# Local attention's 1e-9 as a constant row of the value product, and one bank for the last pooled queries' scores

## The chip, the cores and the metric

The kernel runs on one core of a Trainium2 chip. The metric is the device time of one execution in microseconds, taken as the median of several runs of the same program. Five engines work beside each other, each with its own instruction stream in a fixed order: TensorE (PE in the rows; its weight loads are PEld), VectorE (DVE), ScalarE (ACT), GpSimd (POOL) and SyncE (SP), which here issues most of the DMAs. Matmuls write PSUM, which has eight banks of 128 partitions by 512 fp32 columns.

## The reference

Two attentions over the same q, k and v (4 batches, 8 heads, 576 positions, head size 64) are added, and the sum goes through two token-and-channel mixers. The changed part is in the attentions:

```python
def sm_attn(qq, kk, vv):                      # over 144 pooled positions
    s = scale * np.matmul(qq, kk.transpose(0, 1, 3, 2))
    s = s - np.max(s, axis=-1, keepdims=True)
    a = np.exp(s)
    a = a / (np.sum(a, axis=-1, keepdims=True) + 1e-09)
    return np.matmul(a, vv)
...
out_up = np.repeat(out_d, factor, axis=2)     # factor 4
mask = np.abs(pos[:, None] - pos[None, :]) < factor
scores = np.where(mask, scores, -1000000000.0)
scores = scores - np.max(scores, axis=-1, keepdims=True)
attn = np.exp(scores)
attn = attn / (np.sum(attn, axis=-1, keepdims=True) + 1e-09)
out_local = np.matmul(attn, v)
return (out_up + out_local).astype(np.float32)
```

After it come `x + relu(x @ w_ch1) @ w_ch2` style mixers and a product with sines and cosines; the change does not touch them.

## The kernel before

The attention works on pairs of heads and on quads (two pairs, that is four heads). There are 16 pairs (`n`) and 8 quads (`Q`).

`quad_front(Q)` is the pooled attention of a quad. Its first step multiplies 32-query blocks of pooled q with pooled k: for pair `p` and head `j` of the pair, four blocks `c` of 32 queries fill the 128 partitions of the score tile `sd`, bank `j`, columns `p * 144` (L434). 144 pooled queries are four blocks of 32 and 16 more; the last 32 queries of each head are done by a further matmul (L443) into the columns 288 to 431 of bank `j`, on the partitions of block `2 j + p`. Head `j` reads partitions 64 j to 64 j + 63 of q and k, so the two heads use the two halves of TensorE's rows. The second step takes the maxima on VectorE: one reduce for the four main blocks (L452) and two for the last queries, one for each bank, on 64 partitions each (L460). The third takes the exponentials on ScalarE: four main ones (L468) and two on 64 partitions (L473). Then follow transposes on TensorE (L477, L482), copies on ScalarE, the product with the pooled values (L493 to L500) into the tile `od`, the division on VectorE (L504 to L507), a store, and a load that repeats the rows (`xu`).

`pair_local(n)` is the local attention of a pair in blocks of 32 queries by W = 38 keys. The scores (L533) are reduced and shifted on VectorE (L545, L546) into one of two buffers `pbuf`, of which 38 of 64 columns are used; the rest was set to zero at the start (L328). After the exponential (L553) the transposes (L558) bring a whole buffer, keys on partitions, back to PSUM. The product with the values (L568) has 38 rows of keys; a 65th value column of ones gives the sum of the exponentials. VectorE adds 1e-9 to that sum (L577), takes the reciprocal (L578) and multiplies (L582).

`token_mix`, `token_hidden`, `token_out` are the first mixer over positions (tiles `t1`, `t2`), `mix` the one over channels (tiles `c1`, `c2`).

PSUM is shared by two pools. `big` has two tiles of two banks each (`wide(...)`): all score, transpose and local output tiles. `mmp` has four tiles of one bank (tag `mm`): `od`, `t1`, `t2`, `c1` and `c2`. A tile of a pool waits until an earlier tile's last reader has released its bank.

The order of the work is written out by hand in `ORDER` (L33 to L84): each entry runs one step (the code up to the next `yield`) of a generator. `F` is quad_front, `L` pair_local, `T` token_mix, `E` token_hidden, `U` token_out (which copies `t2` out on ScalarE, L653), `C` mix, `H` and `O` its hidden and output steps. Each engine executes its instructions in exactly that order. Line 42 of it begins:

```
P13 T2 P12 L9 L10 C0 A6 F5 X4 C0 U2.0 L10 U2.0 X5 U2.0 C0 X3 F5 X6 F4 F5 C0 A7 F4 ...
```

Here the first `F5` is the first step of quad 5, and the first `F4` is the seventh step of quad 4, the division.

Of the kernel before, what the change touches and what calls it, by code (L numbers as in the profile page):

```python
# [12 lines left out]
F32 = mybir.dt.float32  # L13
# [5 lines left out]
AF = mybir.ActivationFunctionType  # L19
ALU = mybir.AluOpType  # L20
AX = mybir.AxisListType
# [72 lines left out]
B, H, S, D = 4, 8, 576, 64  # L94
DM = H * D
SD = S // 4
DTOK = 256
# [4 lines left out]
W = 38  # L102
# [12 lines left out]
def kernel(  # L115
# [16 lines left out]
    act, dve, pool, pe, sp = nc.scalar, nc.vector, nc.gpsimd, nc.tensor, nc.sync  # L132

    dram = ctx.enter_context(tc.tile_pool(name="dram", bufs=1, space=DRAM))
    od_d = [[dram.tile([32, 4, DTOK], F32, name=f"od_{b}_{h}") for h in range(2)] for b in range(B)]
    ot_d = [[dram.tile([32, DTOK], F32, name=f"ot_{b}_{h}") for h in range(2)] for b in range(B)]
# [148 lines left out]
    mmp = ctx.enter_context(tc.tile_pool(name="mma", bufs=8 - 2 * WIDE, space=PSUM))  # L285
# [7 lines left out]
    def wide(name):  # L293
        return big.tile([128, 2, 512], F32, tag="big", name=name)
# [28 lines left out]
    def constants():  # L323
        sp.dma_start(fixed, consts)
        yield
        pool.memset(zero, 0.0)
        for t in pbuf:
            pool.memset(t, 0.0)  # L328
        yield
        act.copy(id16, idt)  # L330
        yield
# [50 lines left out]
    def load_values(n):  # L382
        b, p4 = divmod(n, 4)
        vw = sb2.tile([128, 18, 65], F32, tag="vw", name=f"vw_{b}_{p4}")
        for rows in (slice(0, 32), slice(32, W)):
            for j in range(2):
                sp.dma_start(vw[64 * j + rows.start : 64 * j + rows.stop], vloc[b, p4, j, rows])
        values[n] = vw
        yield
# [35 lines left out]
    def quad_front(Q):  # L425
        b, hh = divmod(Q, 2)
        at = f"{b}_{hh}"
        qkd = pooled[Q]
        qd, kd = qkd[:, :, 0], qkd[:, :, 1]
        sd = wide(f"sd_{at}")  # L430
        for p in range(2):
            for c in range(4):
                for j in range(2):
                    pe.matmul(  # L434
                        sd[32 * c : 32 * c + 32, j, p * SD : (p + 1) * SD],
                        qd[64 * j : 64 * j + 64, p, 32 * c : 32 * c + 32],
                        kd[64 * j : 64 * j + 64, p, :],
                        start=True,
                        stop=True,
                    )  # L440
            for j in range(2):
                c = 2 * j + p
                pe.matmul(  # L443
                    sd[32 * c : 32 * c + 32, j, 2 * SD : 3 * SD],
                    qd[64 * j : 64 * j + 64, p, SD - 32 : SD],
                    kd[64 * j : 64 * j + 64, p, :],
                    start=True,
                    stop=True,
                )
        yield  # L450
        mx = sb2.tile([128, 5], F32, tag="mxd", name=f"mxd_{at}")
        dve.tensor_reduce(  # L452
            out=mx[:, 0:4].rearrange("p (j a) -> p j a", j=2),
            in_=sd[:, :, 0 : 2 * SD].rearrange("p j (a n) -> p j a n", a=2),
            axis=AX.X,
            op=ALU.max,
        )
        for j in range(2):
            r = slice(64 * j, 64 * j + 64)
            dve.tensor_reduce(out=mx[r, 4:5], in_=sd[r, j, 2 * SD : 3 * SD], axis=AX.X, op=ALU.max)  # L460
        yield
        scale = 1.0 / (16.0 * math.sqrt(D))
        act.activation(mx, mx, AF.Copy, scale=-scale)
        pd = sb1.tile([128, 5, SD], F32, tag="pd", name=f"pd_{at}")
        for j in range(2):
            for p in range(2):
                i = 2 * j + p
                act.activation(  # L468
                    pd[:, i, :], sd[:, j, p * SD : (p + 1) * SD], AF.Exp, scale=scale, bias=mx[:, i : i + 1]
                )  # L470
        for j in range(2):
            r = slice(64 * j, 64 * j + 64)
            act.activation(pd[r, 4, :], sd[r, j, 2 * SD : 3 * SD], AF.Exp, scale=scale, bias=mx[r, 4:5])  # L473
        yield
        pt = wide(f"pdt_{at}")
        for i in range(5):
# [9 lines left out]
        act.copy(pts[:, 4:7].rearrange("p a n -> p (a n)"), pt[:, 1, 0:384])  # L486
        yield
        vs, vl = pooled[Q, "v"]
        od = mmp.tile([128, 512], F32, tag="mm", name=f"od_{at}")

        rows = [slice(32 * c, 32 * c + 32) for c in range(4)]
        for r in rows:
            pe.matmul(od[r, 0:260], pts[:, 5, r], vl.rearrange("p h d -> p (h d)"), start=True, stop=False)  # L493
# [12 lines left out]
        ods = sb1.tile([128, 5, 64], F32, tag="ods", name=f"ods_{at}")  # L506
        dve.tensor_tensor(out=ods, in0=odv[:, :, 0:64], in1=rd.to_broadcast([128, 5, 64]), op=ALU.mult)  # L507
        yield
        base, tail = od_d[b][hh], ot_d[b][hh]
        sp.dma_start(base.rearrange("s k n -> k s n"), ods[:, 0:4, :].rearrange("p c d -> p (c d)"))  # L510
        sp.dma_start(tail.rearrange("s (c d) -> c s d", c=4), ods[:, 4, :])
        yield
        xu = sb1.tile([128, NB, DTOK], F32, tag="xu", name=f"xu_{b}_{hh}")
        xus[Q] = xu
        src = base.rearrange("s k n -> s (k n)").unsqueeze(1).to_broadcast([32, 4, 4 * DTOK])
        sp.dma_start(xu[:, 0:4].rearrange("p k n -> p (k n)"), src)
        src = tail[16:32].unsqueeze(1).to_broadcast([16, 4, DTOK])
        for j in range(2):
            sp.dma_start(xu[64 * j : 64 * j + 64, 4], src)
        yield  # L520
# [1 line left out]
    def pair_local(n):  # L522
# [9 lines left out]
        for i, j, r, g in groups:  # L532
# [15 lines left out]
            in0=sv,  # L548
# [17 lines left out]
        for i, j, r, g in groups:  # L566
            h = 64 * j
            pe.matmul(  # L568
                o[r : r + 32, 5 * j + i // 2],
                pts[h : h + W, i // 2, r : r + 32],  # L570
                vw[h : h + W, g, :],
                start=True,
                stop=True,
            )
        yield
        rl = sb2.tile([128, 2 * NB, 1], F32, tag="rl", name=f"rl_{at}")
        dve.tensor_scalar(out=rl, in0=o[:, :, 64:65], scalar1=1e-9, scalar2=None, op0=ALU.add)  # L577
        dve.reciprocal(out=rl, in_=rl)  # L578
        if p == 0:
            xs_of[n // 2] = sb2.tile([128, 2, NB, 128], F32, tag="x", name=f"x_{at}")  # L580
        x = xs_of[n // 2]
# [797 lines left out]
def _layout(x):  # L1379
# [6 lines left out]
    vpad = np.zeros((B, 4, 2, S + 6, 65), f)  # L1386
    vpad[:, :, :, 3 : 3 + S, 0:64] = v.reshape(B, 4, 2, S, D)
    vpad[..., 64] = 1.0
    vloc = vpad[:, :, :, np.arange(W)[:, None] + 32 * np.arange(18), :]

    vg = np.ones((B, 2, 2, 2, SD, 4, 65), f)
    vg[..., 0:64] = v.reshape(B, 2, 2, 2, SD, 4, D).transpose(0, 1, 3, 2, 4, 5, 6)
# [42 lines left out]
```

## Time and profile before

| what | value |
| --- | --- |
| time, median of 3 runs | 685.61 us (683.41 to 687.0) |
| profiled execution | 681.57 us, of which the span of its instructions 679.8 us |
| PE (matmul) busy | 655.9 us, 96% of the span, 7320 instructions |
| PEld busy | 626.7 us, 92% |
| DVE busy | 521.0 us, 77%, 952 instructions |
| ACT busy | 321.2 us, 47%, 632 instructions |
| POOL busy | 98.5 us, 14%, 92 instructions |
| chain that ended last | PE 84%, DVE 8%, DMA 3%, ACT 3% |

The attention runs in the first 190 us or so; the channel mixers and the last stage follow. Matmuls are pipelined, so a busy PE is not PE at its peak. A row's idle time in brackets is that of the engine just before the first of its instructions, with what ended it; "issue" means that the engine waited for nothing that the profile shows.

### The profile page before, as it was taken

Reading aid. Unit: us, or ns where it says so; the run is one execution under the profiler, and the core shown is the slowest. Engines: PE = TensorE matmul, PEld = TensorE weight load, DVE = VectorE, ACT = ScalarE, POOL = GpSimd, SP = SyncE. Lnnn points to the kernel's source line nnn. Section 1 sums busy time; section 2 is a strip of 40 time slices with the busy share of each in tenths; the row PEclk is TensorE's granted clock in tenths of the full one; section 3 lists DMA queues with packets and bytes.
Section 4 is the critical chain, followed back from the end, with each engine's and each line's share of the span. In section 5 each row is a group of like instructions: output and inputs, shape, how many; then the busy total and the mean of one; then the engine's idle time right before and its main releaser. Section 6 shows DMA issues by size and latency. Waiting matters only on the chain.

```text
span 679.8 us, 17390 instructions
## 1 busy us (share of the span) xinstructions
PE 655.9 (96%) x7320; PEld 626.7 (92%) x7320; DVE 521.0 (77%) x952; ACT 321.2 (47%) x632; POOL 98.5 (14%) x92
## 2 busy tenths in 40 slices
PE   6769899999999999999999999999999999999997
PEld 4558789889999999999999999999999998998997
DVE  5889998697542888998988867677898748857837
ACT  4566667455341674535434523154647326527311
POOL 3223322305000333300101200012000000000000
PEclk9889999999999999999999999999999999999999
DMA  8787788757343785527263762699410330140202
GB/s 282 239 277 229 250 274 260 252 179 238 110 157 104 242 293 186 202 62 207 66 194 127 209 142 85 238 324 279 130 63 0 112 114 1 62 141 1 71 1 69
DMA packets 93022, 109.93 MB, mean 162 GB/s; under 512 B 46881, under 2 KB 69537, under 8 KB 92945
## 3 DMA queue, kind: packets, MB, share of 16 engines
q1 hardware_dynamic: 92080, 106.08, 49.6%
q0 software_dynamic: 864, 2.75, 1.0%
q8 instruction: 57, 0.93, 0.6%
q14 instruction: 21, 0.16, 0.1%
HBM read 79.13 MB, written 29.69 MB: 160 GB/s over the span
## 4 chain that ended last, share of the span: by engine, by line
PE 84%; DVE 8%; DMA 3%; ACT 3%; SPq 1%; issue 1%; DVEq 0%; ACTq 0%
PE y L157 6%; PE y L158 6%; PE y L159 6%; PE c L157 4%; PE c L158 4%; PE c L159 4%; PE c L699 4%; PE c L702 4%; PE c L700 4%; PE c_p L905 3%; PE c_p L902 3%; PE c_p L903 3%; PE t L157 2%; PE t L159 2%; PE t L158 2%; DMA qk<-qkT 2%
## 5 line engine op out<-in xcount | busy, mean ns | idle before, releaser
L157 PE MATMUL y<-wrh,zh 128*128 128x288 f32 x256 | 75.0, 296 | 0.8 <-ACT zh L151 0.8
L158 PE MATMUL y<-wrl,zh 128*128 128x288 f32 x256 | 74.9, 296 | 0.0
L159 PE MATMUL y<-wrh,zl 128*128 128x288 f32 x256 | 72.9, 295 | 0.0
L219 POOL TENSOR_TENSOR ww<-ww,raw 128x512 int32<-128x512 int32 (+2 forms) x30 | 41.1, 1373 | 159.2 <-DMA raw<-w_ch 52.5
L157 PEld LDWEIGHTS y<-wrh,zh 128*128 128x128 f32 x256 | 48.0, 188 | 1.1 <-ACT zh L151 1.1
L158 PEld LDWEIGHTS y<-wrl,zh 128*128 128x128 f32 x256 | 48.0, 188 | 0.0
L159 PEld LDWEIGHTS y<-wrh,zl 128*128 128x128 f32 x256 | 47.3, 188 | 0.0
L219 POOL TENSOR_TENSOR raw<-raw 128x512 int32<-128x512 int32 (+2 forms) x16 | 20.0, 1249 | 136.7 <-DVE raw L215 74.1
L1212 DVE TENSOR_TENSOR cx<-y,cx 128x288 f32<-128x288 f32 x32 | 14.4, 455 | 30.3 <-PE y L159 29.9
L151 ACT CAST cuh<-cx 128x288 fp32r<-128x288 f32 (+1 forms) x16 | 8.8, 553 | 57.5 <-DVE cx L1212 57.4
L157 PE MATMUL th<-thh,cxh 128*128 128x512 f32 (+1 forms) x92 | 31.6, 343 | 0.0
L158 PE MATMUL th<-thl,cxh 128*128 128x512 f32 (+1 forms) x92 | 31.6, 343 | 0.0
L159 PE MATMUL th<-thh,cxl 128*128 128x512 f32 (+1 forms) x92 | 31.6, 343 | 0.0
L199 ACT ACTIVATE ww<-raw 128x512 f32<-128x512 f32 (+2 forms) x30 | 19.5, 649 | 25.3 <-DVE c1l L223 9.4
L921 DVE SCALAR_TENSOR_TENSOR g<-c,g 128x384 fp32r<-128x384 f32 x40 | 21.1, 550 | 12.9 <-ACT g L918 12.9
L918 ACT ACTIVATE g<-c 128x384 fp32r<-128x384 f32 x40 | 19.1, 490 | 24.4 <-PE c L159 24.3
L201 ACT ACTIVATE raw<-raw 128x512 int32<-128x512 uint32 (+3 forms) x46 | 29.5, 640 | 0.0
L568 PE MATMUL o<-vw,plt 38*32 38x65 f32 x1280 | 18.0, 236 | 6.9 <-issue 3.6
L929 DVE TENSOR_TENSOR ut<-c,ut 128x384 f32<-128x384 f32 x32 | 17.1, 551 | 9.8 <-PE c L702 9.8
L568 PEld LDWEIGHTS o<-vw,plt 38*32 38x32 f32 x1280 | 15.4, 110 | 9.6 <-issue 4.8
L157 PE MATMUL t<-w2h,h 128*128 128x256 f32 (+1 forms) x64 | 21.6, 337 | 0.0
L157 PE MATMUL c<-uh,c1h 128*128 128x384 f32 x64 | 21.4, 334 | 0.0
(390 smaller groups left out, 2266.6 us busy)
## 6 DMA issues: line engine op xcount, KB each, us to landing
raw<-w_ch SPq DMA_DIRECT2D x27, 512.0 KB
qk<-qkT SPq DMA_DIRECT2D x16, 582.0 KB
xT<-ut SPq DMA_DIRECT2D x12, 768.0 KB
vd<-vtok SPq DMA_DIRECT2D x8, 650.0 KB
vw<-vloc SPq DMA_DIRECT2D x32, 146.2 KB
uT<-us SPq DMA_DIRECT2D x16, 288.0 KB
ut<-uT SPq DMA_DIRECT2D x6, 768.0 KB
ut<-xT SPq DMA_DIRECT2D x6, 768.0 KB
```

The lines of the kernel that those rows point to most:

```text
L157: pe.matmul(out, lh, rh, start=start, stop=False, skip_group_check=again)
L158: pe.matmul(out, lh, rl, start=False, stop=False, skip_group_check=again)
L159: pe.matmul(out, ll, rh, start=False, stop=stop, skip_group_check=again)
L201: act.activation(f, words[:, :, 0], AF.Copy, scale=2.0**-29)
L219: pool.tensor_tensor(out=w.bitcast(I32), in0=w.bitcast(I32), in1=f, op=ALU.add)
L568: pe.matmul(o[r : r + 32, 5 * j + i // 2], pts[h : h + W, i // 2, r : r + 32], vw[h : h + W, g, :], start=True, stop=True,)
L699: pe.matmul(ps[:, 0:MIX], h[:, cb % 2, d], h1, start=cb == cbs[0], stop=False)
L700: pe.matmul(ps[:, 0:MIX], l[:, cb % 2, d], h1, start=False, stop=False)
L702: pe.matmul(ps[:, 0:MIX], weight[cb // 2][2][:, cb % 2, d], h2, start=False, stop=cb == cbs[-1])
L902: pe.matmul(ps[:, 0:MIX], h[:, cb % 2, d], h1, start=cb == cbs[0], stop=False)
L903: pe.matmul(ps[:, 0:MIX], l[:, cb % 2, d], h1, start=False, stop=False)
L921: dve.scalar_tensor_tensor(out=h2, in0=ps, scalar=0.0, in1=h1.bitcast(F32), op0=ALU.max, op1=ALU.subtract)
```

## The change

The local attention's buffers `pbuf` get a 39th column of ones, set once at the start; the transposes make it a 39th row, and the values on the host get a 39th row of keys that is zero but for 1e-9 in the column of ones. The product over 39 rows so gives the sum plus 1e-9, and L577 goes. The value loads take one more row in their second part.

In quad_front the last 32 queries' scores of all four heads go into the columns 368 to 511 of the bank of `od`, which is taken at the first step for that; their maxima are one reduce over 128 partitions, their exponentials one instruction. The product with the pooled values later uses the columns 0 to 324 of the same bank.

```diff
@@ constants
         for t in pbuf:
             pool.memset(t, 0.0)
+            pool.memset(t[:, :, W : W + 1], 1.0)
@@ load_values
-        for rows in (slice(0, 32), slice(32, W)):
+        for rows in (slice(0, 32), slice(32, W + 1)):
@@ quad_front
         sd = wide(f"sd_{at}")
+        od = mmp.tile([128, 512], F32, tag="mm", name=f"od_{at}")
+        tail = od[:, 512 - SD : 512]
...
                 pe.matmul(
-                    sd[32 * c : 32 * c + 32, j, 2 * SD : 3 * SD],
+                    tail[32 * c : 32 * c + 32],
                     qd[64 * j : 64 * j + 64, p, SD - 32 : SD],
...
-        for j in range(2):
-            r = slice(64 * j, 64 * j + 64)
-            dve.tensor_reduce(out=mx[r, 4:5], in_=sd[r, j, 2 * SD : 3 * SD], axis=AX.X, op=ALU.max)
+        dve.tensor_reduce(out=mx[:, 4:5], in_=tail, axis=AX.X, op=ALU.max)
...
-        for j in range(2):
-            r = slice(64 * j, 64 * j + 64)
-            act.activation(pd[r, 4, :], sd[r, j, 2 * SD : 3 * SD], AF.Exp, scale=scale, bias=mx[r, 4:5])
+        act.activation(pd[:, 4, :], tail, AF.Exp, scale=scale, bias=mx[:, 4:5])
...
-        od = mmp.tile([128, 512], F32, tag="mm", name=f"od_{at}")
@@ pair_local
-                pts[h : h + W, i // 2, r : r + 32],
-                vw[h : h + W, g, :],
+                pts[h : h + W + 1, i // 2, r : r + 32],
+                vw[h : h + W + 1, g, :],
...
-        dve.tensor_scalar(out=rl, in0=o[:, :, 64:65], scalar1=1e-9, scalar2=None, op0=ALU.add)
-        dve.reciprocal(out=rl, in_=rl)
+        dve.reciprocal(out=rl, in_=o[:, :, 64:65])
@@ the values' layout on the host
-    vloc = vpad[:, :, :, np.arange(W)[:, None] + 32 * np.arange(18), :]
+    vloc = np.zeros((B, 4, 2, W + 1, 18, 65), f)
+    vloc[:, :, :, 0:W] = vpad[:, :, :, np.arange(W)[:, None] + 32 * np.arange(18), :]
+    vloc[:, :, :, W, :, 64] = 1e-9
```

## Rows read from the trace of the kernel before

**Rows 1.** Busy time by stretches: stretch, length, each engine, granted clock, DMA share, GB/s.

```profile
58.00:79.00 21.00, 18.64 (x531) 16.40 (x532) 20.16 (x40) 16.01 (x40) 9.25 (x8) 1.00 0.77 256
79.00:102.00 23.00, 22.10 (x701) 19.46 (x699) 21.84 (x38) 15.17 (x31) 6.43 (x6) 1.00 0.85 270
102.00:190.00 88.00, 87.61 (x1809) 81.18 (x1795) 65.59 (x124) 47.35 (x109) 22.38 (x26) 1.00 0.64 211
190.00:460.00 270.00, 270.00 (x1584) 269.49 (x1583) 206.72 (x367) 117.87 (x214) 40.75 (x29) 1.00 0.57 176
```

**Rows 2.** Instructions of two lines: duration min/median/max in ns, first and last start.

```profile
L577 DVE TENSOR_SCALAR rl<-o x16: 153/161/170, 28.5 to 190.6; 128x10 f32<-128x10 f32 x16
...
L460 DVE TENSOR_REDUCE mxd<-sd x16: 286/300/311, 12.7 to 144.6; 64x1 f32<-64x144 f32 x16
```

**Rows 3.** VectorE's timeline near 62 and 71: start, length, instruction, count.

```profile
62.42 0.61 DVE L460 TENSOR_REDUCE mxd<-sd 64x1 f32<-64x144 f32 x2
...
70.84 0.15 DVE L577 TENSOR_SCALAR rl<-o 128x10 f32<-128x10 f32 x1
71.03 0.22 DVE L578 RECIPROCAL rl<-rl 128x10 f32<-128x10 f32 x1
```

**Rows 4.** ScalarE's timeline near 77.

```profile
76.72 1.20 ACT L468 ACTIVATE pd<-sd,mxd 128x144 f32<-128x144 f32 x4
77.79 0.76 ACT L473 ACTIVATE pd<-sd,mxd 64x144 f32<-64x144 f32 x2
```

**Rows 5.** TensorE's timeline near 26 and near 45.

```profile
26.44 0.86 PE L568 MATMUL o<-vw,plt 38*32 38x65 f32 x65 [2.55 <-issue]
...
45.51 1.49 PE L568 MATMUL o<-vw,plt 38*32 38x65 f32 x80 [3.27 <-DVE pbuf L546]
```

**Rows 6.** SP's timeline near 27.

```profile
27.34 2.11 SPq L387 DMA_DIRECT2D vw<-vloc  x4
```

**Rows 7.** VectorE's timeline near 42.

```profile
42.15 1.56 DVE L595 TENSOR_TENSOR x<-x,xu 128x640 f32<-128x640 f32 x2 [1.94 <-DMA xu<-ot]
```

**Rows 8.** TensorE's timeline near 78.

```profile
78.61 0.77 PE L477 MATMUL pdt<-fixed,pd 128*128 128x128 f32 x5 [0.96 <-ACT pd L473]
```

**Rows 9.** TensorE's timeline near 141.

```profile
141.44 0.39 PE L158 MATMUL t<-xl,w1h 128*128 128x256 f32 x1 [0.32 <-DVE xl L606]
```

**Rows 10.** TensorE's timeline, 99 to 103: quad 5's scores and what follows.

```profile
99.69 0.28 PE L443 MATMUL sd<-qkd 64*32 64x144 f32 x1
...
99.75 0.28 PE L443 MATMUL sd<-qkd 64*32 64x144 f32 x1
...
100.28 0.28 PE L533 MATMUL s<-qk 64*32 64x38 f32 x2
101.38 0.79 PE L533 MATMUL s<-qk 64*32 64x38 f32 x66 [0.82 <-issue]
102.10 0.44 PE L157 MATMUL c<-uh,c10h 128*128 128x384 f32 x1
```

**Rows 11.** ScalarE's timeline near 101: the first copy of U2.0.

```profile
100.90 0.37 ACT L653 COPY us<-t 128x256 f32<-128x256 f32 x1
```

**Rows 12.** TensorE's timeline near 66.

```profile
66.47 0.33 PE L629 MATMUL t<-fixed,x 128*128 128x128 f32 x1
```

**Rows 13.** ScalarE's timeline near 66.

```profile
66.49 0.37 ACT L653 COPY us<-t 128x256 f32<-128x256 f32 x1
```

**Rows 14.** POOL's timeline, 1 to 6.

```profile
1.09 1.21 POOL L328 MEMSET pbuf<- 128x640 f32 x2
5.17 0.80 POOL L219 TENSOR_TENSOR raw<-raw 128x288 int32<-128x288 int32 x1 [2.87 <-DVE raw L215]
```

**Rows 15.** The chain of waits near 78: start, length, what.

```profile
78.18 0.39 ACT pd L473
```

**Rows 16.** Busy time by stretches, where the granted clock was low.

```profile
28.30:35.10 6.80, 5.71 (x141) 3.93 (x134) 6.30 (x14) 2.73 (x7) 2.81 (x4) 0.50 0.79 226
45.30:52.20 6.90, 6.33 (x113) 5.34 (x114) 6.73 (x11) 4.92 (x13) 2.89 (x3) 0.51 0.79 260
```

More of the change, by code (lines that the diff above doesn't have):

```diff
@@ L508, in quad_front @@
         yield
-        base, tail = od_d[b][hh], ot_d[b][hh]
+        base, rest = od_d[b][hh], ot_d[b][hh]
         sp.dma_start(base.rearrange("s k n -> k s n"), ods[:, 0:4, :].rearrange("p c d -> p (c d)"))
-        sp.dma_start(tail.rearrange("s (c d) -> c s d", c=4), ods[:, 4, :])
+        sp.dma_start(rest.rearrange("s (c d) -> c s d", c=4), ods[:, 4, :])
         yield
@@ L516, in quad_front @@
         sp.dma_start(xu[:, 0:4].rearrange("p k n -> p (k n)"), src)
-        src = tail[16:32].unsqueeze(1).to_broadcast([16, 4, DTOK])
+        src = rest[16:32].unsqueeze(1).to_broadcast([16, 4, DTOK])
         for j in range(2):
```

## The prediction

> **What bounds the kernel now.** I read the busy time by stretches first, to see where any engine has room; then the duration of the instructions that go; then the chain of waits, and beside it the timelines of the places where the chain leaves TensorE. The stretches say where a saving can count at all. From 102 us on TensorE is busy 87.61 of 88 us and then 270 of 270 [rows 1]: whatever VectorE or ScalarE saves there is hidden, and only a shift of TensorE's own work reaches the end, one for one. Before 102 us TensorE has holes: 2.36 us of 21 in 58 to 79, 0.90 of 23 in 79 to 102 [rows 1], where VectorE is busy 20.16 and 21.84 us. So attention's first 102 us are the only place where VectorE's and ScalarE's work, which is what the change removes, sets the end, and it does so in pieces. The chain tells which: it runs through the reduces of L460 and the add of L577 near 62 and 71 us, through the exponentials of L473 at 78 us, and is TensorE's own from 78.6 on.
>
> **The change part by part.** *The add of 1e-9 (L577)* goes, 16 instructions of 0.161 us [rows 2]; from start to start one takes 0.19 us (70.84 to 71.03) [rows 3]. The reciprocal L578 then reads the bank itself instead of a small tile. The trace has no reciprocal out of PSUM; L577 is an operation of the same size that reads PSUM and takes 0.161 us, and the reciprocal out of SBUF takes 0.22 [rows 3]. Its extra lies between 0 and, at worst, the 0.16 of a whole further pass (which would leave 0.03 of the 0.19); below nothing I exclude, since the elements are the same. I take 0.02, near the L577 row, so 0.17 saved each. [...]
>
> *The second reduce (L460) and the second exponential (L473)* go in each of 8 quads. The pair of reduces takes 0.61 us [rows 3], one 0.300 [rows 2]: 0.30 saved. The pair of exponentials takes 0.76, end to end, one half of it [rows 4]: 0.38 saved. The merged ones do twice the partitions over the same 144 columns; L468 does 128 x 144 in the same time as L473 does 64 x 144 (x4 in 1.20 us) [rows 4]. Off the path and on it this makes 16 x 0.17 + 8 x 0.30 = 5.1 us of VectorE and 3.0 us of ScalarE.
>
> *What of it is on the path.* Before 58 us: nothing. TensorE stands 2.55 us until 26.44 in an "issue" gap, that is on nothing the other engines do [rows 5]; SP's next loads wait for those very matmuls and are then issued one behind another, four in 2.11 us from 27.34 on [rows 6]; and VectorE itself waits 1.94 us for the load of xu at 42.15 [rows 7]. What VectorE and ScalarE gain ahead of that, they spend in those three waits. Bounds: 0 to 1.4 us (two quads' L460 and L473 stand ahead of that load, 2 x 0.68); I take 0, because each of the three waits is ended by something that none of the removed instructions starts. From 58 to 78.6 us: VectorE runs without a gap and carries one L460 (62.42) and one L577 (70.84): 0.30 + 0.17. ScalarE then ends the stretch with L473, for which TensorE waits 0.96 us at 78.61 [rows 4, 8]: 0.38. Sum 0.85 us. TensorE was free at 78.61 - 0.96 = 77.65, and its work before that comes earlier with VectorE too, so it still waits for ScalarE. Bounds 0.4 (POOL and VectorE meet differently) to 1.1. At 141.44 us TensorE waits 0.32 us for a chain of VectorE that holds one L577 [rows 9]: 0.17, bounds 0 to 0.32. Together 1.0 us earlier.
>
> *The tail's bank.* od is now taken from the four mm banks in the first step of quad_front, not the sixth, and held until the seventh (L507). Counting takes and releases along ORDER, no more than four are ever in use before; after, a fifth is asked for once: at F5's first step (ORDER line 42, "A6 F5 ... U2.0") od of quad 4 and three outputs of token_mix 2 still hold all four. The first tail matmul must wait for U2.0's copy. In the times of before, that matmul starts at 99.69 [rows 10] and the copy ends at 100.90 + 0.37 = 101.27 [rows 11]: a stall of 1.58 us. Queued behind it on TensorE, in order, are the other scores of this quad, the 80 score matmuls of the next local pair (L533) and the first channel product (L157, 102.10); no other engine loses by it, because VectorE comes to these scores only at 102.2. But the same stretch already holds a gap of TensorE, from the L533 pair at 100.28 (second start about 100.33) to 101.38, 1.05 us from start to start, put down to "issue" [rows 10]: the next instructions were not there. In the stall they have 1.58 us to arrive, so I count the gap as covered. The work itself, without the gap, is 2.41 - 1.05 = 1.36 us; so L157 comes at 101.27 + 1.36 = 102.63 plus some hundredths for the semaphore, 0.6 late. Both ends of this wait move earlier together by what was gained before, since the copy stands behind the load of the first mix's input, which hangs on the same work. I take 0.6; bounds: 0 if the copy gains more than the matmul does, 1.6 if the gap stays behind the stall.
>
> One other bank gets tight: t2_0_1_1 starts at 66.47 [rows 12] and would take the bank whose copy ends at 66.49 + 0.37 = 66.86 [rows 13]. That copy stands behind L473 and L460 on its engine and comes about 0.5 earlier with them, and TensorE is not the bound there: 0, bounds 0 to 0.4. Everywhere else the bank was released ahead of its next use, as before.
>
> *The constant row.* The two memsets of 10 elements follow two of 640 that take 1.21 us together [rows 14]; POOL is then idle 2.87 us until 5.17 [rows 14], which hides anything up to that: 0 (uncovered, at most another 1.2). The values' second load has 7 rows for 6, 4.7 KB in 146 KB a pair: 0, bounds 0 to 0.2. Contracting over 39 partitions for 38 changes no column count: 0; the 65 columns of L568 set its time.
>
> *Sum:* -0.85 - 0.17 + 0.6 = -0.4 us. The profiled execution took 681.57 us (span 679.8 and 1.8 around it), so 681.2 of this kind; the median of the three runs is 685.61, 4 us above it, and the same 0.4 less makes **685.2 us**. Three runs of the same program spread over 683.4 to 687.0, so what a measurement of this kernel can tell from no change is about 0.5%, 3.4 us.
>
> **The rivals.**
> *The stall is paid in full.* The instruction gap follows the stall instead of lying in it: +1.6 for +0.6, sum +0.6, 686.2 us. For it: nothing in the profile says when those instructions were asked for. Against: the gap stood right behind the block of small matmuls that runs through the same place.
> *The stall is free and more of the chain gives.* L460 three times, L577 twice and L473 twice lie on the chain of before, the last of the seven at 78.18 [rows 15]: 0.90 + 0.34 + 0.76 = 2.0, and 0.17: 683.4 us. Against it the three waits named above, before 58 us.
> *Everything removed counts:* 5.1 + 3.0 us, 677.5 us. For it VectorE is 96% busy from 58 to 79 [rows 1]; against it TensorE's full stretches after 102.
> [...]
> *Slower: the tail's matmuls stand in line.* The four tail matmuls of a quad come from both halves of the array's rows; before they wrote two banks (j), now one. The matmuls of a half take 0.28 us each [rows 10] and start under 0.1 apart; one behind another they would cost some 0.8 us more a quad, on the path in three quads (F5, F6, F7): +2.4, sum +2.0, 687.6 us. [...] No row of before has that pattern; here the four write different partitions, so I give it little.
>
> **How the numbers follow.** Forecast 0.55, stall in full 0.13, chain gives more 0.18, everything counts 0.03, clock 0.07, in line 0.04. The first three all lie within 0.5%; with the spread of the runs (1.8 us to either side of the middle) the chain rival and the forecast put 0.08 below 682.2, with everything-counts 0.10. Above 689.0 lie most of the clock's chance and 0.02 of the spread: 0.08. Same: 0.82. The range that leaves out 2 in 10 is 682.2 to 688.4; the forecast's own cost bounds alone (-1.4 to +1.2 on the path after 58 us) would give 684.2 to 686.8.
>
> **What would show it.** Right: TensorE's wait at 78.6 still ended by the exponential, about 0.85 earlier; at about 99 us a wait of some 1.6 us in front of L443's first tail matmul, ended by L653, with no "issue" gap in L533 behind it; L157 of the first channel product within 0.5 us of 102.10; TensorE full from there on. Wrong: a second stall on an mm bank, a granted clock of 0.5 after 99 us, a reciprocal far over 0.22 us, or tail matmuls that start 0.28 apart.

## The result: 1.2% slower, where no change was forecast

Before: 685.23 us, median of 6 executions (682.28 to 687.0). After: 691.98 us, median of 6 (688.82 to 697.03). The ratio is 1.0117, 95% interval 1.0083 to 1.0152, so about 7 us are lost; a second set of executions of both (label r_after) gave 1.0098 (1.0061 to 1.0136). The forecast was 685.2 us, with 0.08 for slower.

The profiled execution after took 697.03 us (span 694.9), the slowest of the six, so its sums are larger than the median's loss. Busy time by the stretches of [rows 1]:

```profile
58.00:79.00 21.00, 15.52 (x479) 12.87 (x470) 17.45 (x33) 14.26 (x34) 9.85 (x8) 0.98 0.71 235
79.00:102.00 23.00, 21.41 (x507) 19.55 (x491) 18.42 (x33) 13.12 (x31) 5.82 (x5) 0.87 0.65 198
102.00:190.00 88.00, 83.23 (x1862) 75.59 (x1857) 63.74 (x113) 43.39 (x99) 24.45 (x27) 0.98 0.65 212
190.00:460.00 270.00, 268.73 (x1742) 267.94 (x1743) 201.66 (x355) 115.92 (x214) 37.27 (x26) 1.00 0.54 167
```

TensorE now idles 5.5 us of 21, 1.6 of 23 and 4.8 of 88, where before it idled 2.4, 0.9 and 0.4; and the granted clock, 1.00 throughout before, is below 1 in all three. VectorE is less busy as well: it waits for TensorE (over the whole span 8.1 us ahead of the reciprocal below, where L577 waited 5.4 before). The loss lies mostly between 60 and 160 us: in the 20 profiles of this study the time up to the matmul that stands at 60.38 us in before is 59.5 to 63.2 us, with no tie to the saving (c_hold, without it, 62.9), and from the one at 160.04 us to the end it is 519.7 to 521.2. Four places stand out in between. The removed instructions are not among them; groups of instructions (busy us, mean ns), against [rows 2, 3]:

```profile
L574 DVE RECIPROCAL rl<-o 128x10 f32<-128x10 f32 x16 | 3.4, 215 | 8.1 <-PE o L565 8.1
L461 DVE TENSOR_REDUCE mxd<-od 128x1 f32<-128x144 f32 x8 | 2.4, 297 | 0.0
L472 ACT ACTIVATE pd<-od,mxd 128x144 f32<-128x144 f32 x8 | 3.2, 399 | 0.0
```

A reciprocal out of PSUM takes what one out of SBUF took (0.215 for 0.22), the maximum over 128 partitions what one over 64 took (297 for 300 ns), and the one exp about half of the pair (0.40 for 0.76 us).

*Place 1, F4's scores, 78 us.* TensorE's timeline:

```profile
73.66 0.48 PE L437 MATMUL sd<-qkd 64*32 64x144 f32 x16
73.93 0.44 PE L446 MATMUL od<-qkd 64*32 64x144 f32 x4
78.35 0.73 PE L437 MATMUL sd<-qkd 64*32 64x144 f32 x16 [3.99 <-issue]
```

TensorE stops for 3.99 us in the middle of the scores, on nothing that another engine does. What "issue" is can be read from the DMA. The list of DMA queues of the changed kernel (queue, kind, packets, MB, share of 16 engines) has one of kind "instruction", q8, and before had the same line:

```profile
q8 instruction: 57, 0.93, 0.6%
```

57 packets make 0.93 MB, 16 KB each; TensorE's stream has 14,746 instructions in the trace, some 259 to a packet. Counting TensorE's instructions in order of time, 77 of the 78 "issue" gaps of over 0.5 us between 10 and 200 us, in the 20 profiles of this study, stand at instruction 194 or 195 plus a multiple of 256 (place 1 at 12 x 256 + 194), and in all 77 TensorE goes on 1.1 to 1.7 us behind the landing of a q8 packet: it waits for its next piece of code. Piece k is here the one that begins at instruction k x 256 + 194, and TensorE crosses into it when it starts that instruction.

In all 20 profiles the packets of pieces 1 to 13 start behind TensorE's crossing into the piece before, by 0.45 to 4.9 us; those of some later pieces start ahead of it (up to 1.9 us at piece 15). The profile counts them on the same 16 DMA engines as the loads. Here the crossing into piece 11 is at 71.07 us. The queues from 71.1 to 75.7 us, then from 75.7 to 76.9 (packets, MB, share):

```profile
q1 hardware_dynamic: 433, 1.32, 78.7%
```

```profile
q1 hardware_dynamic: 35, 0.04, 9.3%
q8 instruction: 1, 0.02, 5.4%
```

The packet of piece 12 starts at 75.80 us, 4.7 behind the crossing, when 1.32 MB of loads have gone through; it is in at 76.83 and TensorE goes on 1.5 later. Before, the crossing was at 68.16 and the packet at 68.74, 0.6 behind. What changed is which came first. SP's timeline before:

```profile
68.14 0.33 SPq L656 DMA_DIRECT2D uT<-us  x1
68.56 0.38 SPq L396 DMA_DIRECT2D vd<-vtok  x1
69.04 1.25 SPq L516 DMA_DIRECT2D xu<-od  x1
```

and after:

```profile
69.25 0.33 SPq L652 DMA_DIRECT2D uT<-us  x1
69.67 0.38 SPq L397 DMA_DIRECT2D vd<-vtok  x1
70.15 0.58 SPq L513 DMA_DIRECT2D xu<-od  x1
```

vd (650 KB) and xu (512 KB) are issued behind U0.0's store, which waits for ScalarE's copies. These stand behind quad 3's maximum and exp, which are now 0.30 and 0.38 us shorter. Counted from the qk load ahead of it (64.37 and 66.53 us), the store comes after 3.8 us before and 2.7 now. Before, TensorE crossed 0.4 us ahead of the issue of vd; after, 1.4 behind it.

*Place 2, F5's first tail matmul*, the stall of the prediction; against [rows 10]:

```profile
111.25 0.32 PE L446 MATMUL od<-qkd 64*32 64x144 f32 x2 [2.38 <-ACT us L649]
```

*Place 3, the first product of token_mix 4 and the first of a later c1 bank.* In the built program the first takes the bank of the fourth c2 product, whose addition stands behind xl (L602) on VectorE; before, it took the bank of the second. The second takes a bank that the hidden layer (L639) frees; before, it took that of quad 6's od. Neither waited before:

```profile
154.07 0.36 PE L157 MATMUL t<-xh,w1h 128*128 128x256 f32 x1 [1.14 <-ACT xs L606]
...
165.62 0.44 PE L157 MATMUL c<-uh,c10h 128*128 128x384 f32 x1 [0.90 <-DVE h L639]
```

*Place 4, the clock behind places 1 and 2* (granted clock in the third column from the end):

```profile
78.10:84.90 6.80, 6.55 (x120) 6.33 (x120) 3.38 (x7) 1.68 (x6) 2.00 (x2) 0.50 0.84 234
112.20:115.60 3.40, 3.40 (x72) 3.31 (x60) 3.30 (x8) 2.46 (x7) 0.00 (x0) 0.50 0.89 265
```

### The profile page after: what moved, and what is told of

Its sections match the earlier page's. It is cut to its first block, busy times and chain, and to the rows that moved or that the text cites. A ratio compares the mean times of both kernels' runs of the same rounds, so it can differ in the third digit from the quotient of the medians.

```text
span 694.9 us, 17362 instructions
## 1 busy us (share of the span) xinstructions
PE 662.7 (95%) x7320; PEld 632.1 (91%) x7320; DVE 516.7 (74%) x928; ACT 317.4 (46%) x624; POOL 99.5 (14%) x94
## 3 DMA queue, kind: packets, MB, share of 16 engines
q1 hardware_dynamic: 92144, 106.23, 48.8%
## 4 chain that ended last, share of the span: by engine, by line
PE 84%; DMA 6%; DVE 5%; issue 2%; ACT 2%; SPq 1%; DVEq 0%; ACTq 0%
PE y L157 5%; PE y L158 5%; PE y L159 5%; PE c L157 4%; PE c L158 4%; PE c L159 4%; PE c L695 4%; PE c L698 4%; PE c L696 4%; PE c_p L901 3%; PE c_p L899 3%; PE c_p L898 3%; PE t L157 2%; PE t L158 2%; PE t L159 2%
## 5 line engine op out<-in xcount | busy, mean ns | idle before, releaser
L530 PE MATMUL s<-qk 64*32 64x38 f32 x1280 | 16.2, 207 | 6.6 <-issue 6.6
L530 PEld LDWEIGHTS s<-qk 64*32 64x32 f32 x1280 | 13.7, 106 | 9.1 <-issue 9.0
L565 PE MATMUL o<-vw,plt 39*32 39x65 f32 x1280 | 19.2, 241 | 2.9 <-issue 1.5
L565 PEld LDWEIGHTS o<-vw,plt 39*32 39x32 f32 x1280 | 16.3, 113 | 6.0 <-issue 3.1
```

What stands on the lines that cost most here:

```text
L530: pe.matmul(s[r : r + 32, j, i // 2 * W : i // 2 * W + W], q[64 * j : 64 * j + 64, 32 * g : 32 * g + 32], k[64 * j : 64 * j + 64, 32 * g : ...
L565: pe.matmul(o[r : r + 32, 5 * j + i // 2], pts[h : h + W + 1, i // 2, r : r + 32], vw[h : h + W + 1, g, :], start=True, stop=True,)
```

## The experiments

Ratios are to the kernel before on the same chip, with 95% intervals. The last columns come from the one profiled execution of each kernel, in us: d, by how much more time than before lies between the same two TensorE matmuls (those at 60.38 and 160.04 us in the first profile of before, 99.66 apart); p12, the delay of piece 12's packet behind its crossing; gap, TensorE's wait for that piece; rest, its waits of over 0.3 us for pieces 10 to 27 otherwise; F5, T4 and c1, the bank waits of places 2 and 3 (over 0.3 us; T4 with the wait for xl behind it); low, time at the lower clock from 58 to 200 us. TensorE's other waits are not in the table.

```
label      ratio   interval          d   p12  gap rest   F5  T4  c1   low
before     -       -               0.0   0.6  0.0  0.8  0.0 0.3 0.0   0.0
b_again    0.9990  0.9960-1.0020   1.2   1.7  0.0  0.0  0.0 0.0 0.0   0.0
a_const    1.0002  0.9974-1.0031  -0.4   0.8  0.0  0.4  0.0 0.0 0.0   0.0
c_hold     0.9992  0.9964-1.0019   0.0   0.9  0.0  0.0  0.0 0.0 0.0   0.0
g_touch    1.0070  1.0039-1.0101   6.6   1.0  0.0  0.0  1.9 0.9 1.1   3.4
k_merge    1.0023  0.9993-1.0053   2.2   3.7  1.5  0.0  0.0 0.0 0.0   6.8
e_own      1.0007  0.9982-1.0033   9.4   3.9  2.6  1.9  2.7 0.3 0.0   6.8
b_tail     1.0072  1.0042-1.0102   6.9   2.8  0.9  0.0  3.2 1.1 1.1   6.8
after      1.0117  1.0083-1.0152  11.8   4.7  4.0  2.1  2.4 1.1 0.9  10.2
r_after    1.0098  1.0061-1.0136   7.9   3.2  1.5  1.6  2.4 1.1 0.9   6.8
h_last     1.0103  1.0054-1.0152   4.3   2.6  1.0  0.0  2.2 1.5 0.9   3.4
f_order    1.0111  1.0069-1.0153   7.4   4.2  3.2  3.2  0.0 1.1 0.9   3.4
v_later    1.0090  1.0057-1.0123   3.9   1.8  0.1  0.4  0.5 1.0 0.9   3.4
t_add      1.0096  1.0060-1.0131   8.5   3.5  2.3  0.6  2.8 0.4 0.9   6.8
all3       1.0108  1.0067-1.0149   5.1   2.7  1.0  2.3  0.0 0.4 0.9   3.4
mend       1.0066  1.0032-1.0100   2.2   1.5  0.0  0.8  1.1 0.4 0.9   0.0
skip57     1.0050  1.0013-1.0087  -0.6   2.3  0.4  0.0  0.0 0.0 0.0   0.0
skip357    1.0055  1.0020-1.0090   4.1   1.1  0.0  2.0  0.0 0.0 0.0   6.8
only57     1.0022  0.9998-1.0046   7.7   0.6  0.0  1.5  2.8 0.4 1.1   3.4
own_const  1.0056  1.0028-1.0084   3.4   3.5  1.8  2.5  0.0 0.0 0.0   3.4
```

One profile is one execution out of a spread of some 5 to 12 us, so a row tells which waits a kernel has; what it costs is told by the ratio. e_own's profile is the slowest of its 12 executions (689.98 us, median 686.73), skip57's the fastest (682.93, median 689.46).

### Which part of the change loses

*a_const:* the constant row alone.

```diff
+            pool.memset(t[:, :, W : W + 1], 1.0)
...
-        dve.tensor_scalar(out=rl, in0=o[:, :, 64:65], scalar1=1e-9, scalar2=None, op0=ALU.add)
-        dve.reciprocal(out=rl, in_=rl)
+        dve.reciprocal(out=rl, in_=o[:, :, 64:65])
```

> Only the constant row: the 39th row of probabilities and values and the reciprocal read straight from PSUM; the pooled scores as before. Theory 1 (the loss comes from the pooled tail taking its bank at the scores): 684 to 686 us, like before, with no wait of TensorE for U2.0's copy in F5 and the granted clock at 0.5 for about 14 us as before. Theory 2 (the loss comes from the constant row: 78 KB more of DMA and later instruction code): 690 to 694 us, the whole loss. Theory 3 (any change of the instruction order moves the code-fetch gaps of TensorE and the clock falls with them): 685 to 692, its own pattern of gaps.

1.0002: alone it costs and gives nothing that an interval of 0.3% either way can tell. Theory 2 falls as far as the row stands alone.

*b_tail:* the shared tail alone (the hunks of quad_front).

> Only the shared tail bank; local attention as before (with its 1e-9 addition). Theory 1 (bank taken at the scores): 690 to 694 us, the whole loss, with TensorE waiting 1.5 to 2.5 us for U2.0's copy before F5's first tail matmul and one or two more clock falls of about 3.4 to 6.8 us. Theory 2 (constant row): 684 to 686. Theory 3 (moved code-fetch gaps): anywhere from 685 to 692.

1.0072, two thirds of the loss, with F5's wait of 3.2 us.

*c_hold:* od's bank taken early, nothing written.

```diff
         sd = wide(f"sd_{at}")
+        od = mmp.tile([128, 512], F32, tag="mm", name=f"od_{at}")
...
-        od = mmp.tile([128, 512], F32, tag="mm", name=f"od_{at}")
```

> The kernel before with one edit: the bank of the pooled product od is taken at the scores, but nothing is written to it before the products; tail scores, maxima and exps as before. If theory 1's loss comes from the bank being away from the rotation: 690 to 694 us. If it comes from the stall of the tail's matmuls on that bank (theory 1b), or from tail matmuls of two row halves running into one bank (theory 4): 684 to 687, since no matmul of the scores meets the bank here. Theory 2: 685.

0.9992: a tile that is only taken early does no harm here. Its place among the four banks came out differently too (in the built program quad 5's od takes the bank that U2.0's second copy frees, with a tail the first copy's), so this is no pure test of holding.

*e_own:* the shared tail in a tile of its own, od late.

```diff
+        tail = mmp.tile([128, 512], F32, tag="mm", name=f"tl_{at}")[:, 0:SD]
```

> The shared tail in a bank of its own from the same pool of four, freed after its exp; od taken late, as before; local attention as before. Theory 1b (stall at the tail's first matmul in F5 behind U2.0's copy) and theory 4 (two row halves into one bank): 689 to 694 us, as with od's own bank, since the first write is at the same place. Theory 1 (bank held too long): 685 to 688, as it is given back some 6 us earlier. Theory 2: 685.

1.0007, against 1.0072 with od's bank, although its profile has F5's wait (2.7 us) and the code gap. It has neither wait of place 3. Theory 1b expected the loss of b_tail here; so F5's wait and the clock fall behind it (3.4 us) are in this kernel, and 12 executions show next to no loss. Theory 1 expected this result, but missed c_hold's.

*r_after:* the changed kernel again.

> The changed kernel once more, for a second profile and a narrower ratio: 690 to 694 us, F5's wait of 2 to 3 us and a clock fall behind it by theory 1b; theory 3 says that the gap in F4 need not come back at 4.0 us.

The gap in F4 came back at 1.52 us, F5's wait at 2.42, place 3 unchanged.

### The wait alone, the saving alone

*g_touch:* the kernel before with od early and one more matmul into it.

```diff
+            if p == 0:
+                pe.matmul(od[0:32, 512 - SD : 512], qd[0:64, 0, SD - 32 : SD], kd[0:64, 0, :], start=True, stop=True)
```

> The kernel before with od's bank taken at the scores and one additional tail matmul (32 columns of weights, 144 moving) into it between the scores of p = 0 and the tails; everything else, the two maxima and the two exps too, as before. So it has the wait in F5 without the merge. Theory 1b: the wait of 2 to 3 us and the clock fall after it come back, 688 to 690 us. Theory 4 (tail matmuls of both row halves in one bank cost time) or theory 3: 684 to 686 us with no clock fall behind F5.

1.0070, with two exps and two maxima as before and, from 58 us on, not one code gap of over 0.3 us:

```profile
101.78 0.31 PE L443 MATMUL od<-qkd 64*32 64x144 f32 x1 [1.86 <-ACT us L654]
```

So taking the bank early and writing it loses some 5 us without the saving. Its profile has the waits of places 2 and 3 and the clock fall behind F5; that these are the 5 us is argued, and e_own and only57, which have F5's wait and the fall as well, lose less. Theory 4 (both row halves in one bank) is not needed for this loss: this matmul stands alone in its bank.

*k_merge:* only the saving. The one maximum and the one exp read 144 columns of the main scores, so this kernel leaves out the tail's own probabilities.

```diff
+        dve.tensor_reduce(out=mx[:, 4:5], in_=sd[:, 1, 0:SD], axis=AX.X, op=ALU.max)
...
+        act.activation(pd[:, 4, :], sd[:, 1, 0:SD], AF.Exp, scale=scale, bias=mx[:, 4:5])
```

> The kernel before with only the saving: one maximum and one exp over 128 partitions instead of two of each over 64, od's bank taken late as before. To need no shared bank they read 144 columns of the main scores in the tail's place, so the tail's probabilities are not the reference's. Theory 5 (a faster VectorE and ScalarE send vd's 650 KB and xu's 512 KB about 1 us earlier, before TensorE asks for its code piece 12, and TensorE then waits 1 to 4 us for that piece in F4's scores, with a clock fall behind it): 686 to 688 us, the packet of piece 12 starts 2.5 to 4.7 us behind the crossing into piece 11, and not 0.6 to 1.0 us as in the four kernels with two exps; no wait in F5 and none at T4's first product. Rival (the code gap belongs to the tail's bank): 683 to 685 us, no gap in F4.

```profile
73.36 0.47 PE L443 MATMUL sd<-qkd 64*32 64x144 f32 x4
75.35 0.73 PE L434 MATMUL sd<-qkd 64*32 64x144 f32 x16 [1.52 <-issue]
```

```profile
74.90:81.70 6.80, 6.35 (x119) 6.12 (x119) 4.98 (x10) 3.64 (x10) 2.90 (x3) 0.50 0.69 197
```

The packet of piece 12 starts 3.7 us behind its crossing, the gap is there at the same instruction, and the clock falls, with no bank taken early: the gap in F4 comes from the saving, as theory 5 says. In time it shows little: 1.0023, which may be nothing. In the seven profiles with two exps in quad 3 (before twice, a_const, c_hold, g_touch, skip357, only57) the packet's delay is 0.6 to 1.7 us and there is no gap at piece 12. In the 13 with one exp it is 2.3 to 4.7 us with a gap of 0.4 to 4.0; the exceptions are mend and v_later (1.5 and 1.8, no gap), where loads were put later. all3 has v_later's edit too, but 2.7 us and a gap of 1.0. The order on SP fits: counted from the load of raw (L187) two issues ahead, U0.0's store comes 4.5 to 4.6 us later in those seven profiles and in mend, 3.6 to 3.8 in the other twelve. vd is issued 0.1 to 0.4 us behind TensorE's crossing in six of the seven and in mend (in skip357 0.3 ahead), and 0.5 to 1.4 us ahead of it in the ten others that have it in its old place.

*h_last:* the four tail matmuls behind both groups of scores.

```diff
+        for p in range(2):
             for j in range(2):
                 c = 2 * j + p
```

> The changed kernel with the four tail matmuls behind both groups of 16 scores and not behind each. If the loss sits in TensorE's going to and fro between sd's and od's banks (theory 4) or in the code gap behind F4's first tails (theory 3, which then lies elsewhere): 686 to 689 us. Theory 1b: the wait in F5 begins 0.2 to 0.4 us later and ends at the same copy, so 690 to 692 us.

1.0103 with F5's wait at 2.18 us: theory 1b as it said; going to and fro between banks is not what costs.

### Moving the waits away

*f_order:* F5's scores behind U2.0's copies.

```diff
-C0 A6 F5 X4 C0 U2.0 L10 U2.0 X5 U2.0 C0
+C0 A6 X4 C0 U2.0 L10 U2.0 F5 X5 U2.0 C0
```

> The changed kernel with F5's scores (quad 5's first step) put behind U2.0's two copies in the written order; nothing else. Theory 1b (the loss is F5's wait for its bank, 2.4 to 3.2 us in three profiles, and the clock fall of 3.4 us that follows it, worth half of that): TensorE no longer waits for U2.0's copy, no clock fall at 106 to 116 us, and 4 us less than the changed kernel: 687 to 689 us. Theory 3 (code-fetch gaps, the one of 0.9 to 4.0 us in F4's scores above all): 690 to 693, the gap in F4 is still there.

F5's wait and its clock fall are gone, and nothing is won (1.0111), where theory 1b expected 4 us. Two code gaps stand in the same stretch, 2.03 us and, at 106.88, 0.81; the second lies where the one of before did [rows 10], which the wait had covered in both profiles of the change.

```profile
103.43 0.76 PE L530 MATMUL s<-qk 64*32 64x38 f32 x64 [2.03 <-issue]
```

*v_later:* vd of quad 4 behind U0.1's store.

```diff
-F3 L4 U0.0 V4 K9 F2 F3 X0 L6 L4 L6 T1 F4 U0.1 X0 F3 T1 L5 U0.1 X0 T1 U0.1 F4
+F3 L4 U0.0 K9 F2 F3 X0 L6 L4 L6 T1 F4 U0.1 X0 F3 T1 L5 U0.1 X0 T1 U0.1 V4 F4
```

> The changed kernel with the load of vd for quad 4 (650 KB) put behind U0.1's store in the written order, some 6 us later. Theory 5: the packet of code piece 12 starts at least 1.5 us sooner behind its crossing, the gap in F4 is under 1 us, and the time is 1 to 3 us under the changed kernel's: 688 to 690. If the load in front of the code packet doesn't matter: 690 to 693 us; slower still if vd then comes too late for the value sums.

The packet starts 1.8 us behind its crossing (4.7 and 3.2 with the load in front), the gap is 0.05 us, as expected. But all3, with the same edit, has 2.7 and 1.0 us; in both xu's load (512 KB) is issued 0.5 to 0.6 us ahead of the crossing. So the load's place matters, and vd's alone does not decide it. A later product now waits, and the time stays (1.0090):

```profile
87.59 0.55 PE L625 MATMUL t<-fixed,x 128*128 128x128 f32 x3 [1.86 <-ACT us L649]
```

*t_add:* the c2 addition ahead of xl.

```diff
-X28 C0 T4 X28 T4 F7 O0.3 O0.2 L12
+X28 C0 O0.3 T4 X28 T4 F7 O0.2 L12
```

> The changed kernel with the addition of the fourth c2 product to ut put ahead of xl on VectorE, so that the bank that T4's first product takes comes free some 1.5 us sooner. Theory 6 (the bank held from the scores on makes T4's first product wait 1.1 us for that addition, and the hidden layer behind it 0.9 us): 1 to 2 us under the changed kernel's time, 688 to 690.5 us, with T4's first product waiting for nothing. If those two waits lie beside others: no difference, 690 to 692 us.

T4's first product no longer waits, its second waits 0.39 us for xl, and c1's wait stays at 0.92. 1.0096: no gain that can be measured, where theory 6 expected 1 to 2 us.

*all3:* these three edits together.

> The changed kernel with three places mended at once: F5's scores behind U2.0's copies, vd of quad 4 behind U0.1's store, the fourth c2 addition ahead of xl. If the loss of 7 us is F5's bank wait (2.9 us with its clock fall), the code gap in F4 (about 2) and T4's bank wait (1.8), and nothing takes their places: 684 to 686 us. If code gaps come in the place of F5's wait, as where F5 alone was moved: 687 to 689 us.

1.0108, above both expectations. The gap in F4 is still 0.97 us, L625 waits 1.59 us as in v_later, and a code gap of 1.57 us stands in L530; that these take what was won is not shown.

*mend:* f_order's and t_add's edits, and U0.0's second copy behind quad 3's two copies of transposed probabilities (the expectation calls them quad 2's), which puts the loads back by 1 us.

```diff
-X2 X0 U0.0 F3 L4 U0.0
+X2 X0 F3 U0.0 L4 U0.0
```

> The changed kernel with F5's scores behind U2.0's copies, the fourth c2 addition ahead of xl, and U0.0's second copy behind quad 2's two copies of transposed probabilities on ScalarE, which puts vd's and xu's loads 1.1 us later again, to where they were. If the three waits are the loss and these moves bring no others: 684 to 687 us. If a code gap again takes the place of F5's wait (2.0 us where F5 alone was moved): 687 to 690 us.

1.0066, the lowest ratio of the kernels with the whole change, though its interval meets theirs: no gap in F4, F5's wait 1.13 us, no clock fall after 58 us. It is still slower than before.

### Taking quads out

*skip57, skip357:* quads 5 and 7, or 3, 5 and 7, by the code of before.

```diff
+        late = Q in (5, 7)
+        od = None if late else mmp.tile([128, 512], F32, tag="mm", name=f"od_{at}")
...
+        od = mmp.tile([128, 512], F32, tag="mm", name=f"od_{at}") if late else od
```

> The changed kernel with quads 5 and 7 as before (tails in sd's two banks, two maxima and exps, od's bank taken late); the other six quads and local attention as changed. If F5's bank wait (2.9 us) and the waits of T4's and c1's first products (1.1 and 0.9 us, from quad 7's early bank) are the loss but for the code gap in F4: 685 to 688 us, no wait for U2.0's copy, T4's first product without a wait, the code gap in F4 still there. If the loss is spread or comes from the constant row together with the tail: 689 to 692 us.

> The same with quad 3 as before too, whose shorter maximum and exp let vd's and xu's loads start ahead of code piece 12. Three causes make up the whole loss: 683 to 686 us, as before, and the packet of code piece 12 starts 0.6 to 1.1 us behind its crossing with no gap of over 0.5 us in F4's scores. If the start of the packet doesn't go back: 685 to 688 us, as without quads 5 and 7.

The waits of places 2 and 3 are gone in both. 1.0050 and 1.0055: about half of the loss, by the middles of intervals of 0.3 to 0.4%. Quad 3 changes piece 12's packet as expected (1.1 us, no gap), but not the time; its profile has a gap at another piece and a clock fall behind it:

```profile
104.23 0.79 PE L542 MATMUL s<-qk 64*32 64x38 f32 x66 [1.52 <-issue]
```

*only57:* the shared tail in quads 5 and 7 alone, no constant row.

```diff
+        late = Q in (0, 1, 2, 3, 4, 6)
```

> The kernel before with the shared tail bank in quads 5 and 7 alone; local attention as before. F5's bank wait (2 to 3 us; with what follows 2.9 us) and the bank waits of T4's and c1's first products (1.1 and 0.9 us): 688.5 to 691 us, no code gap in F4's scores beyond 0.5 us, and a clock fall behind F5. If the loss with quads 5 and 7 as before (3.5 us) and this don't add up to 7 to 8 us but this shows nearly nothing: 685 to 687 us.

1.0022, below what was expected, with F5's wait at 2.81 us, the clock fall behind it (3.4 us) and c1's wait (1.08 us) in the profile. T4's first product does not wait: in this program, whose quad 6 takes its bank late, it has the bank of the first c2 product.

```profile
107.03 0.31 PE L446 MATMUL od<-qkd 64*32 64x144 f32 x2 [2.81 <-ACT us L661]
```

0.22% and 0.50% add up to 0.72%, against 0.98 and 1.17% for the whole; with intervals of 0.25 to 0.4% that is no contradiction, but it leaves up to 3 us unassigned.

*own_const:* e_own with the constant row.

> The constant row together with the shared tail in a bank of its own that is freed after the exp. If the rest of the loss needs od's bank to be held until the products: 684 to 688 us, like the constant row alone (685.6 by its ratio) and the own bank alone (685.9). If the constant row costs 2 to 3 us as soon as the tail is shared: 688 to 690 us. F5's wait for U2.0's copy is there in either case.

1.0056, where the own bank alone had 1.0007 and the row alone 1.0002. The row costs something once the tail is shared, as the second expectation said. F5's wait, expected in either case, is not in its profile. The profile has code gaps of 1.80 us in F4 and 2.46 ahead of F5's scores; that these are the row's doing is not shown.

*b_again:* the kernel before.

> The kernel before once more, for a second profile: 683 to 687 us. By the theory of the code packets, no gap of over 0.5 us in F4's scores and a packet of piece 12 that starts 0.6 to 1.1 us behind its crossing, no wait of T4's first product, and 14 to 21 us at the lower clock, all of it before 60 us.

0.9990. No wait of places 1 to 3; the packet's delay was 1.7 us, over the 1.1 expected, without a gap. But a copy of L653 (token_out's) can hold TensorE here without the change too, and the clock did not fall behind this wait:

```profile
103.00 0.44 PE L157 MATMUL c<-uh,c10h 128*128 128x384 f32 x1 [1.50 <-ACT us L653]
```

## Why the prediction was wrong, point by point

- *Durations of the edits:* right, each within 0.03 us; the 0.02 us that the prediction took for a reciprocal out of PSUM does not show (0.215 us against 0.216 out of SBUF, on average). So was their being hidden before 58 us, for the constant row: a_const, with all 16 additions gone, is the time of before.
- *"From 58 to 78.6 us ... 0.85":* this step failed, and by its sign. The sum took the earlier ScalarE and VectorE for an earlier TensorE, and did not ask what SP would issue earlier by them. What they released was 1.2 MB of loads, ahead of a code packet that TensorE needed (k_merge, v_later). From the matmul at 60.38 us to the one at 78.61 before took 18.2 us (b_again 17.9), the change 23.5 and 19.8, k_merge 21.2; mend and v_later, which have the saving without the gap, took 16.7 and 16.8 (one profile each). So the saving is there, 1.1 to 1.5 us, and what the sum lacked is the code gap. The wait for the exp at 78.6, which was to stay, is in neither profile of the change. In the five profiles with two maxima and two exps in every quad waits for pieces 10 to 27 sum to 0 to 0.8 us; in the two of the change to 6.1 and 3.1.
- *F5's stall:* place, releaser and the covered "issue" gap came as forecast (no code gap in L530 behind it in either profile of the change; f_order shows it when the wait is gone). The term of 0.6 us was mis-sized: the wait is 2.4 us for 1.58, and 3.4 us at a granted clock of 0.50 follow. Between the matmuls at 98 and 104 us of before the delay of TensorE grows by 3.0 us (r_after 2.9). That is against one execution of before: in b_again, where TensorE waits for a copy of L653 later on, the same stretch takes 1.8 us more than in before. And the profile does say when code was fetched, against the first rival: the packets of q8 have times.
- *"Everywhere else the bank was released ahead of its next use":* this failed too. Place 3's two waits, 1.1 and 0.9 us, are of banks that the early od of quads 6 and 7 displaced; both are in g_touch and b_tail, c1's alone in only57 (quad 7 early, quad 6 late), and neither is in e_own or where quads 5 and 7 take od late (skip57, skip357). I counted how many banks were live, not which bank each tile would get and whose release that was.
- *The clock* (0.07, most of it above 689.0) was nearest. Before, the granted clock was 0.50 for some 6.8 us from 28.3 and again from 45.3 on [rows 16], behind standstills of 2.55 and 3.27 us [rows 5]. As long a fall behind F5's stall I estimated from these at 3.4 us, half of the 6.8, with the stall's 0.6 at 689.6 us in all; its condition was the code gap behind the stall, for a standstill as long as those two. The gap was covered, and a fall of 3.4 us came all the same, behind 1.9 us in g_touch.
- *The rival of matmuls in line* did not come: each tail matmul of the program is two instructions in the trace, and the four of a pair, from both row halves, start 0.01 to 0.14 us apart in one bank where the granted clock is 1.00 (four in 0.44 us, where one takes 0.28; place 1's rows), as they did in two (0.02 to 0.12).
- *Constant row, 0:* right alone, though its loads carry 150 KB more in all (q1 106.08 and 106.23 MB), twice what the prediction's 4.7 KB a pair and the expectation's 78 KB say; with the shared tail not (own_const, and the change against b_tail: 1.0117 and 1.0098 against 1.0072, which intervals alone would allow). The product over 39 rows took what the one over 38 took (0.217 us, the median of 1280).

What is shown: the bank taken early and written loses some 5 us without the saving (g_touch), and brings the waits at F5, T4 and c1; the saving moves a code packet behind the loads (k_merge, v_later, mend), at no cost that can be measured alone (1.0023). What stays open: how the 5 us divide among the waits, for F5's wait and the fall behind it show next to no loss in e_own and little in only57, and how the last 2 to 3 us come about. Taking out the quads with the waits gives back about half, moving them away 0.3 to 0.5% at best (mend), and code gaps turn up at other pieces. No version with the shared tail is shown to be faster than the kernel before.

## What to carry to other kernels

Before an engine off the critical path is made faster, look at what it releases on the DMA queue: here loads that started earlier stood in front of a piece of TensorE's own code, whose packet started 3.7 us behind its crossing in k_merge and 0.6 and 1.7 in the two profiles of before. A PSUM tile that is taken earlier brought here not only its own first wait (2.38 us at F5) but two of other tiles (1.14 and 0.90 us, place 3): look up which bank every later tile then gets, and whose release that is. A wait on TensorE should be priced with the code gap that it covers and with the clock behind it: without F5's wait and its clock fall f_order had code gaps of 2.03 and 0.81 us in the same stretch, and won nothing (1.0111).

## What the runs showed of the hardware

- TensorE's code came in packets of 16 KB (57 packets, 0.93 MB, some 259 of its 14,746 instructions to one), and 77 of the 78 "issue" gaps of over 0.5 us stood at instruction 194 or 195 plus a multiple of 256. The packet of piece 12 started 0.6 to 4.7 us behind the crossing, later where loads were issued ahead of it, and TensorE went on 1.1 to 1.7 us behind a packet's landing in all 77 places where it had waited over 0.5 us. At place 1 it ran through the 256 instructions in 3.0 us (71.07 to 74.1), and the next piece took 7.3 to be there.
- The granted clock fell to 0.50 for 3.4 us behind F5's wait in each of the eight profiles with a wait of 1.9 to 3.2 us there, not behind 1.1 us in mend; but behind the 2.0 us at 103.43 in f_order it did not. Behind 1.50 us in b_again it did not fall, behind 1.52 us in k_merge it was low for 6.8 us. In these profiles the length of one standstill does not decide it.
- The tails of both row halves, which write different partitions of one bank, started 0.01 to 0.14 us apart at a granted clock of 1.00, about as close as before in two banks (0.02 to 0.12), and up to 0.21 us apart at 0.50 (before 0.19); what happens inside the bank no trace shows.
